# Grouped DoubleRow matmuls, norms spread through DRAM, and a merged last load group in a fused attention and feed-forward kernel

## The chip, the cores and the metric

The kernel runs on one core of a Trainium2 chip. In the profiles PE is TensorE, which does the matmuls, and PEld its weight loads; the program puts their results in PSUM banks (`g_ps`, `v_ps` and others, two of each of these). DVE (VectorE), ACT (ScalarE) and POOL (GpSimd) do the element-wise work, SP issues DMAs. A DMA "lands" when its data has arrived, and "[0.30 <-X]" after a line says that the engine sat idle for 0.30 us before it, until X ended. The metric is the device time in microseconds of one execution. The profile of an execution also gives its span, from the first to the last instruction, which is some 1.8 us shorter than the time.

## The reference

```python
qn = q / (norm(q, axis=1) + 1e-6)          # q, k, v: (4, 6016, 256), tau = 1
kn = k / (norm(k, axis=1) + 1e-6)
s = kn.transpose(0, 2, 1) @ qn / tau       # 256 x 256 per batch
a = softmax(s)                             # over the last axis
x = (v @ a).reshape(24064, 256)
out = (silu(x @ w_gate) * (x @ w_val)) @ w_out     # 256 -> 1536 -> 256
```

## The kernel before

The kernel folds the attention matrix into the feed-forward weights (`Wg`, `Wv`), so the main loop is three matmul groups per step: `g_ps`, `v_ps` (512 columns each, two matmuls each) and four of the output product `o_new` (256 columns). ScalarE makes `silu`, VectorE multiplies it with `v_ps`. A step takes 1.30 us of TensorE.

Beside these steps, a plan spreads the next batch's attention over the loop: squares for the norms, the raw product of q and k in fp8 (`gemm1_pair`, with DoubleRow, a mode in which one fp8 matmul takes two 128-row blocks), the norms, the logits, the softmax, the new weights. The parts that the change touches:

```python
def gemm1_pair(b, t):                     # one pair of 128-row blocks, two halves
    ...
    for jh in range(CH):
        nc.tensor.matmul(kq[:, jh, :], q_sb[:, ps:ps + 2, js], k_sb[:, ps:ps + 2, :],
                         ..., perf_mode=DR)          # the last block alone: plain fp8

def norm_cols(b):                         # sums of squares -> inverse norms, one per partition
    ...
    nc.gpsimd.tensor_tensor(out=inv, in0=inv, in1=minus, op=ALU.pow)
    state[b, "inv"] = inv
    parts = split3(inv[:, CH:], [P, CH], "ink")      # three bf16 parts
    ...                                              # and back to fp32 scalars, "scal"
def norm_diag(b):                         # 6 scaled identities on VectorE
    ...
def norm_rows(b):                         # 3 matmuls: ones x diag = k's norms in every row
    for i in range(3):
        nc.tensor.matmul(ps, ones_bf, state[b, "diag"][:, i], start=(i == 0), stop=(i == 2))
    nc.vector.tensor_copy(ink, ps)

for t in range(NP):                       # 24 pairs per batch
    step = SQ0 + (5 * t) // 2
    plan[step].append((norm_acc, t))
    plan[step + 1].append((gemm1_pair, t))
...
plan[S1 + 10].append((norm_cols,))
plan[S1 + 20].append((norm_diag,))
plan[S1 + 22].append((norm_rows,))
plan[S1 + 24].append((logits, 0))
```

The first batch has nothing to hide behind. Its k and q are loaded in groups, squared, multiplied and summed as they land. The v and weight loads queue behind them.

## Time and profile before

| | before |
|---|---|
| time, median of 3 runs | 815.24 us (815.13 to 815.67) |
| span of the profiled run | 813.4 us, granted clock 1.0 |
| TensorE busy | 98% |
| VectorE, ScalarE, GpSimd busy | 65%, 53%, 33% |
| TensorE idle before the first use of w_gate's second part | 0.30 us at 40.68 us |

A matmul's duration in this profile is its latency, and matmuls overlap, so what one costs in a full stream is the distance between starts: 216 ns for 512 columns, 109 ns for 256.

### The profile page before, as it was taken

How to read it: one execution, taken by the hardware profiler on the slowest of the kernel's cores; microseconds unless marked ns; L12 is line 12 of the kernel's file. 1: busy time of each engine (PE TensorE's matmuls, PEld its weight loads, DVE VectorE, ACT ScalarE, POOL GpSimd, SP SyncE). 2: the span in 40 equal slices, each digit the busy share in tenths (PEclk: the TensorE clock that was granted, in tenths of full speed). 3: DMA queues.
4: the chain of work that ended last, by engine and by line, in shares of the span. 5: the costliest groups of instructions: out<-in, count | busy, mean ns of one | idle time of the engine just before them, and what ended most of it. 6: DMA issues, size and time to landing. Idle time of an engine off the chain costs nothing.

```text
span 813.4 us, 13803 instructions
## 1 busy us (share of the span) xinstructions
PE 800.5 (98%) x5051; PEld 487.1 (60%) x5051; DVE 526.9 (65%) x816; ACT 434.9 (53%) x757; POOL 266.9 (33%) x345
## 2 busy tenths in 40 slices
PE   5999999999999999999999999999999999999998
PEld 3656666665565666666565666666656565665656
DVE  4777777667556777756756687765765555555554
ACT  4666655545555656545555566555554544544543
POOL 5515887313000888722000398751300000000000
PEclk9999999999999999999999999999999999999999
DMA  9993875328312678333813278532662112112101
GB/s 87 142 160 69 112 105 88 78 53 122 79 40 46 96 101 105 75 65 87 127 40 59 38 101 119 92 78 66 139 98 66 46 47 59 53 39 65 50 27 59
DMA packets 93507, 64.59 MB, mean 79 GB/s; under 512 B 52752, under 2 KB 92304, under 8 KB 92688
## 3 DMA queue, kind: packets, MB, share of 16 engines
q0 software_dynamic: 19344, 27.01, 28.6%
q1 hardware_dynamic: 73952, 36.65, 18.5%
q8 instruction: 39, 0.64, 0.3%
q14 instruction: 28, 0.23, 0.1%
q10 hardware_dynamic: 144, 0.07, 0.0%
HBM read 78.64 MB, written 36.70 MB: 142 GB/s over the span
## 4 chain that ended last, share of the span: by engine, by line
PE 95%; DMA 4%; POOL 0%; issue 0%; DVE 0%; POOLq 0%
PE o_new L474 30%; PE g_ps L440 30%; PE v_ps L440 30%; DMA q_sb<-in_q_dram 2%; PE ps L409 2%; PE kq_new L151 2%; DMA k_sb<-in_k_dram 1%; DMA w_gate_sb<-in_moe_w_gate_dram 1%; POOL k_sb L106 0%; PE last_ps L498 0%; PE ps L334 0%; PE cs L308 0%; POOL w_val_sb L541 0%; PE kq_new L156 0%; POOL vb L114 0%
## 5 line engine op out<-in xcount | busy, mean ns | idle before, releaser
L450 DVE TENSOR_TENSOR sv<-silu,v_ps 128x512 bf16<-128x512 bf16 (+1 forms) x576 | 388.7, 675 | 262.6 <-ACT silu L446 260.8
L446 ACT ACTIVATE silu<-g_ps 128x512 bf16<-128x512 f32 (+1 forms) x576 | 338.5, 588 | 324.8 <-PE g_ps L440 299.3
L474 PE MATMUL o_new<-w_out_sb,sv 128*128 128x256 bf16 x2244 | 337.3, 273 | 0.0
L440 PE MATMUL g_ps<-vT,Wg 128*128 128x512 bf16 (+1 forms) x1128 | 331.3, 375 | 0.0
L440 PE MATMUL v_ps<-vT,Wv 128*128 128x512 bf16 (+1 forms) x1128 | 330.4, 375 | 0.0
L474 PEld LDWEIGHTS <-sv 128*128 128x128 bf16 x2244 | 219.1, 98 | 141.1
L440 PEld LDWEIGHTS <-Wv 128*128 128x128 bf16 x1152 | 112.5, 98 | 130.8
L284 POOL TENSOR_TENSOR acc_new<-acc_new,sq 128x512 f32<-128x512 f32 x135 | 158.0, 1170 | 43.2 <-DVE sq L274 33.8
L440 PEld LDWEIGHTS <-Wg 128*128 128x128 bf16 x1152 | 106.6, 98 | 27.1
L274 DVE TENSOR_TENSOR sq<-q_sb 128x512 bf16<-128x512 fp8e5 x72 | 64.5, 896 | 0.0
L279 POOL TENSOR_TENSOR acc_new<-sq 128x512 f32<-128x512 bf16 x3 | 3.5, 1152 | 150.6 <-DVE sq L274 150.6
L275 ACT ACTIVATE sq<-k_sb 128x512 bf16<-128x512 fp8e5 x72 | 44.2, 614 | 0.0
L151 PE MATMUL kq_new<-k_sb,q_sb 128*128 128x512 fp8e5 x184 | 40.1, 310 | 0.7 <-DMA q_sb<-in_q_dram 0.7
L483 ACT COPY o_sb<-o_new 128x512 f32<-128x512 f32 x48 | 28.1, 585 | 14.9 <-PE o_new L474 14.5
L106 POOL DMA_DIRECT2D q_sb<-in_q_dram x49 | 27.5, 561 | 13.6 <-DMA k_sb<-in_k_dram 5.4
L485 DVE COPY o_sb<-o_new 128x512 f32<-128x512 f32 (+1 forms) x47 | 31.3, 666 | 0.0
L106 POOL DMA_DIRECT2D k_sb<-in_k_dram x48 | 26.1, 550 | 12.1 <-DMA w_out_sb<-in_moe_w_out_dram 5.3
L178 PE MATMUL ss_new<-sq,ones_bf 128*128 128x256 bf16 x83 | 17.8, 353 | 9.3 <-ACT sq L168 8.7
L114 POOL DMA_DIRECT2D vb<-in_v_dram x47 | 24.2, 516 | 4.1 <-DMA vb<-in_v_dram 3.3
L151 PEld LDWEIGHTS <-q_sb 128*128 128x256 fp8e5 x184 | 22.2, 138 | 3.2 <-DMA q_sb<-in_q_dram 2.2
L178 PEld LDWEIGHTS <-ones_bf 128*128 128x128 bf16 x83 | 9.9, 122 | 16.0 <-issue 11.6
L354 POOL TENSOR_SCALAR den<-th 128x512 f32<-128x512 f32 x3 | 1.8, 609 | 51.8 <-ACT th L353 51.8
(101 smaller groups left out, 205.9 us busy)
## 6 DMA issues: line engine op xcount, KB each, us to landing
out_dram<-o_sb SPq DMA_DIRECT2D x92, 256.0 KB, 2.4
vb<-in_v_dram POOLq DMA_DIRECT2D x43, 256.0 KB, 5.5
k_sb<-in_k_dram POOLq DMA_DIRECT2D x44, 128.0 KB, 6.0
q_sb<-in_q_dram POOLq DMA_DIRECT2D x44, 128.0 KB, 5.0
w_out_sb<-in_moe_w_out_dram POOLq DMA_DIRECT2D x1, 768.0 KB, 13.5
vb<-in_v_dram POOLq DMA_DIRECT2D x4, 192.0 KB, 3.7
vT<-vb SPq DMA_TRANSPOSE x47, 4.3
w_gate_sb<-in_moe_w_gate_dram POOLq DMA_DIRECT2D x2, 256.0 KB, 7.0
```

The lines of the kernel that those rows point to most:

```text
L106: nc.gpsimd.dma_start(out=dst[:, gs:gs + gm, :], in_=src[b].rearrange("(p s) c -> p s c", s=NS)[:, gs:gs + gm, :])
L151: nc.tensor.matmul(kq[:, jh, :], q_sb[:, ps:ps + 2, js], k_sb[:, ps:ps + 2, :], start=(t == 0 and jh == 0), stop=last, perf_mode=DR, skip_ ...
L178: nc.tensor.matmul(state[b, "ss", which], ones_bf, sq[:, s, :], start=(t == 0 and s == 0), stop=(t == t_last and s == pm - 1))
L274: nc.vector.tensor_mul(sq[:, :pm, 0, :], q_sb[:, ps:ps + pm, :], q_sb[:, ps:ps + pm, :])
L275: nc.scalar.activation(sq[:, :pm, 1, :], k_sb[:, ps:ps + pm, :], ACT.Square)
L284: nc.gpsimd.tensor_tensor(out=acc, in0=acc, in1=sq[:, s, :, :], op=ALU.add)
L440: nc.tensor.matmul(dst[:, :mv], W[:, kk, fs], vT[:, kk, :mv], start=(kk == 0), stop=(kk == CH - 1))
L446: nc.scalar.activation(silu[:, :mv], g_ps[:, :mv], ACT.Silu)
L450: nc.vector.tensor_mul(sv[:, f, :mv], silu[:, :mv], v_ps[:, :mv])
L474: nc.tensor.matmul(self.o_ps[:, j % 2, :], self.sv[:, f, j * P:(j + 1) * P], w_out_sb[:, f, :], start=(f == 0), stop=(f == FH - 1))
L483: nc.scalar.copy(o_sb[:, :m, :], self.o_ps[:, :m, :])
L485: nc.vector.tensor_copy(o_sb[:, :m, :], self.o_ps[:, :m, :])
```

## The change

It has three parts: two pairs of the q-k product are issued together; k's inverse norms reach all partitions by a write to DRAM and a broadcast read, in place of scaled identities and three matmuls; and in the first batch the last two groups of q are handled as one, so that all q-k matmuls precede the last column sums.

```diff
         state[b, "inv"] = inv
-        parts = split3(inv[:, CH:], [P, CH], "ink")
-        ...                                  # scal, norm_diag and norm_rows go
+        row = dram.tile([C], FP32, tag="ink_row")
+        nc.gpsimd.dma_start(out=row.rearrange("(h p) -> p h", p=P), in_=inv[:, CH:])
         ink = work.tile([P, C], FP32, tag="ink")
-        nc.vector.tensor_copy(ink, ps)
+        nc.gpsimd.dma_start(out=ink, in_=row.partition_broadcast(P))
...
         plan[step].append((norm_acc, t))
-        plan[step + 1].append((gemm1_pair, t))
+        if t % 2 == 1:
+            plan[step + 1].append((gemm1_pair, t - 1))
+            plan[step + 1].append((gemm1_pair, t))
...
-    plan[S1 + 20].append((norm_diag,))
-    plan[S1 + 22].append((norm_rows,))
...
-        ts = range(gs // 2, (gs + gm + 1) // 2)
+        ts = list(range(gs // 2, (gs + gm + 1) // 2))
+        if which == 0 and g == NQ - 1:
+            continue
+        if which == 0 and g == NQ - 2:
+            gs, gm = gl[g + 1]
+            ts += range(gs // 2, (gs + gm + 1) // 2)
```

More of the change, by code (lines that the diff above doesn't have):

```diff
@@ L315, in norm_cols @@
         state[b, "inv"] = inv
-        parts = split3(inv[:, CH:], [P, CH], "ink")
-        scal = work.tile([P, 3, CH], FP32, tag="scal")
-        for i, part in enumerate(parts):
-            nc.gpsimd.tensor_copy(scal[:, i, :], part)
-        state[b, "scal"] = scal
-    def norm_diag(b):
-        scal = state[b, "scal"]
-        diag = work.tile([P, 3, CH, P], BF16, tag="diag")
-        for i in range(3):
-            for h in range(CH):
-                nc.vector.tensor_scalar_mul(diag[:, i, h, :], in0=ident,
-                                            scalar1=scal[:, i, h:h + 1])
-        state[b, "diag"] = diag
-    def norm_rows(b):
-        ps = psum_m.tile([P, C], FP32, tag="misc")
-        for i in range(3):
-            nc.tensor.matmul(ps, ones_bf, state[b, "diag"][:, i], start=(i == 0),
-                             stop=(i == 2))
+        row = dram.tile([C], FP32, tag="ink_row")
+        nc.gpsimd.dma_start(out=row.rearrange("(h p) -> p h", p=P), in_=inv[:, CH:])
         ink = work.tile([P, C], FP32, tag="ink")
-        nc.vector.tensor_copy(ink, ps)
+        nc.gpsimd.dma_start(out=ink, in_=row.partition_broadcast(P))
         state[b, "ink"] = ink
```

## The prediction

> **What bounds the kernel now.** I read the page first: the busy shares, then the chain that ended last, then the waits.
>
> ```profile
> span 813.4 us, 13803 instructions
> PE 800.5 (98%) x5051; PEld 487.1 (60%) x5051; DVE 526.9 (65%) x816; ACT 434.9 (53%) x757; POOL 266.9 (33%) x345
> ...
> PE 95%; DMA 4%; POOL 0%; issue 0%; DVE 0%; POOLq 0%
> ```
>
> TensorE is busy for 98% of the span and is 95% of the chain that ended last; DMA is 4%, all of it before 41 us. VectorE and GpSimd, where much of the change works, are at 65% and 33%. Busy alone doesn't say that TensorE runs without gaps, so I looked at its timeline in a stretch where the next batch's q-k product (L151) runs beside the feed-forward part:
>
> ```profile
> 66.64 0.60 PE L474 MATMUL o_new<-w_out_sb,sv 128*128 128x256 bf16 x4
> 66.99 0.46 PE L151 MATMUL kq_new<-k_sb,q_sb 128*128 128x512 fp8e5 x2
> 67.30 0.61 PE L440 MATMUL g_ps<-vT,Wg 128*128 128x512 bf16 x2
> 67.74 0.59 PE L440 MATMUL v_ps<-vT,Wv 128*128 128x512 bf16 x2
> 68.17 0.60 PE L474 MATMUL o_new<-w_out_sb,sv 128*128 128x256 bf16 x4
> 68.61 0.60 PE L440 MATMUL g_ps<-vT,Wg 128*128 128x512 bf16 x2
> 69.04 0.59 PE L440 MATMUL v_ps<-vT,Wv 128*128 128x512 bf16 x2
> 69.47 0.60 PE L474 MATMUL o_new<-w_out_sb,sv 128*128 128x256 bf16 x4
> ```
>
> The first column is the start, the second the busy time; the durations overlap, so starts are to be compared. A step without L151 goes from 68.17 to 69.47, 1.30 us. A step with it goes from 66.64 to 68.17, 1.53 us. So one pair of L151 matmuls costs 0.23 us, in full, on the engine that sets the end. I then compared, over all records from 40.6 us to the end, the distance between consecutive matmul ends with the rate given below. It fits within a nanosecond on average except in three kinds of place: one wait at 40.68 us (0.30 us), a surcharge of 15.1 ns in the mean each of 69 times when TensorE goes from L151 to g_ps, and some ten to twenty ns after each group of one-column matmuls. From 41 us on, therefore, a matmul that is taken away shortens the run by its spacing, and work on the other engines is free until it delays TensorE. Before that, a DMA ends the chain:
>
> ```profile
> 34.10 6.53 DMA w_gate_sb<-in_moe_w_gate_dram
> 40.68 1.04 PE ps L409 x4
> ```
>
> **What the Trainium skill says.** "TensorE: Matmul & The Clock Gate", section "Wait — 56ns, not 53.3ns?", gives a warm spacing of N ÷ 2.4 GHz + about 2.5 ns: 109.2 ns for 256 columns, 215.8 ns for 512. The trace agrees: four of 512 and four of 256 make 1.300 us, the step measured above. The same page, "Weight-path perf modes", says that DoubleRow's weight load takes 72% longer and turns the fast load off. The trace shows 138 ns against 98 ns, 41% longer. With four in a row at the start of the kernel (33.76 us, 0.63 us for four, of which the first one's own time is 0.30) the spacing is still 0.11 us, so the longer load doesn't show inside a run of them. "DMA: Bandwidth & Descriptors", "Two DMAs through the same engine are not ordered", asks for the first DMA's completion before the second is issued. The built program does this on GpSimd's queue. Its "Anatomy of one DMA" gives about 2.0 us fixed cost; the trace's smallest stores (64 KB) land in 1.5 to 2.0 us and its loads, often queued, in 4 to 6.
>
> **Part 1, two pairs of the q-k product at a time.** The number of matmuls stays the same: 23 DoubleRow pairs and one last half pair per batch, three batches. Only the returns from DoubleRow to bf16 become fewer. Before, 69 returns × 15.1 ns = 1.04 us. Afterwards the instruction order shows 12 groups per batch, of which 11 end with a DoubleRow pair and the last ends with the plain half pair (whose return costs nothing in the trace). That removes 33 returns for certain, and the three last ones if the change from DoubleRow to plain fp8 is free: 33 to 36 × 15.1 ns = **0.50 to 0.54 us**. The 0.44 us group itself can't starve anything: each g and v bank has a twin. The even pairs no longer lengthen their own step, which takes 0.23 us from the slack between the read of a v bank and its reuse; in the steady state the least of these slacks at a step concerned is 0.53 us (v_ps at 479.6 us), so 0.30 us remains.
>
> **Part 2, the inverse norms by way of DRAM.** It removes these groups:
>
> ```profile
> L327 DVE TENSOR_SCALAR diag<-ident,scal 128x128 bf16<-128x128 bf16 x18 | 3.2, 247 | 0.0
> L334 PE MATMUL ps<-diag,ones_bf 128*128 128x256 bf16 x9 | 1.5, 273 | 0.0
> L337 DVE COPY ink<-ps 128x256 f32<-128x256 f32 x3 | 1.3, 417 | 0.0
> L319 POOL CAST scal<-lo 128x2 f32<-128x2 bf16 x3 | 0.6, 190 | 0.0
> ```
>
> (columns: count, then busy us and mean ns of one, then idle before). On TensorE it is 9 matmuls, and their worth is the spacing, not the 273 ns latency: 9 × 109.2 ns = **0.98 us**. The 4.5 us of VectorE and some 4 us of small GpSimd operations lie beside TensorE and are worth nothing. Added are two DMAs per batch. GpSimd ends the last power at 166.96 us in the first batch; VectorE first reads the norms at 183.05 us. The window is 16.1 us, and 15.7 once the three matmuls of L334 between them are gone. Two legs, each an issue of about 0.6 us and a landing of 2 to 6 us (read from the loads and stores above, and one behind the other), come to 5 to 13 us. So the landing is expected at 172 to 180 us, unseen. The v load behind them on GpSimd slips by a few us; its transposed tile has about 24 us between landing and first use.
>
> **Part 3, the first q's last two groups as one.** TensorE does the last q-k product before the column sums, so one or two mode changes go, perhaps 0.03 to 0.1 us up to the softmax. But every gain up to 40.4 us runs into the w_gate transfer shown above, which landed at 40.63 us and was issued when an earlier load had landed, whatever TensorE does. TensorE already waits 0.30 us for it; it would only wait longer. Worth **0**.
>
> Sum: 0.98 + 0.52 + 0 = 1.5 us, so 815.24 − 1.5 = **813.7 us**, 0.2%.
>
> **Rivals.** (a) The norms arrive late. VectorE is in order, so its first logits operation would hold up the product behind it, and TensorE would stop once the two v banks are full. For it: many 4-byte writes to DRAM, one DMA that must land before the next is issued, and a queue shared with loads. Against: the window of nearly 16 us, and no load outstanding on that queue at 167 us (the load before landed at 155.5). If each landing took 10 us, the norms would come at 188 us, 5.5 us late; the second bank hides about 1 us of it, and three batches lose 13.5 us: 827 us. I give it 4%. (b) The surcharge belongs to each DoubleRow pair and not to the return, or grows with a longer run because 138 ns loads can't keep up with 109 ns matmuls. Part 1 would then be worth nothing or cost up to 36 × 30 ns: 814.3 to 815.3 us. The four in a row at the start speak against it. (c) The start counts after all, because the w_gate landing shifts between runs: then up to 0.1 us more goes, 813.6 us. (d) More slack on VectorE and GpSimd speeds up TensorE: there are no gaps it could fill, so nothing.
>
> **Range and chances.** The three runs before spread over 0.54 us, all of which can come from the loads at the start. A spread of this kind on both sides and 0.5 us for rival (b) give 813.1 to 814.7 us. Two per cent is 16.3 us; no sum of the parts comes near it, and only a much worse rival (a) reaches it upward. Faster by over 2%: 0.5%; within 2%: 98%; slower: 1.5%.
>
> **What would show it.** TensorE's count should fall by 9, to 5042. No group with diag or scal should be left. A step holding two pairs should take 1.30 + 0.45 us (four × 109.2 + 15 ns) and the steps between 1.30. The wait for w_gate near 40.7 us should stay, longer by what the softmax gained. The broadcast norms should land by 180 us, and the logits should have no wait for a DMA before them. I am wrong if VectorE waits for a DMA at the logits, if TensorE shows gaps near 183, 378 and 573 us, if a double group costs more than 0.47 us, or if the time before 41 us moves by more than 0.5 us.

## The result

The changed kernel took 813.64 us in the median of 6 runs (813.54 to 814.2), the kernel before 815.34 us in 6 runs. The ratio is 0.998 (95% interval 0.9967 to 0.9993). Ratios here are the mean time of one kernel's fast runs over that of the other's in the same rounds, so they are not quite the ratio of the medians. By the limit of 2% the two are the same. The predicted time was 813.7 us.

From the page of the changed kernel (span; busy time, share and instruction counts; the engines' shares of the chain that ended last):

```profile
span 811.9 us, 13668 instructions
...
PE 794.1 (98%) x4952; PEld 488.9 (60%) x5042; DVE 524.3 (65%) x795; ACT 434.8 (54%) x757; POOL 267.2 (33%) x330
...
PE 93%; DMA 4%; issue 1%; DVE 1%; POOL 0%; ACT 0%; POOLq 0%
```

The span is 1.5 us shorter. There are 9 weight loads fewer (5051 to 5042), as there should be matmuls. Of the matmuls themselves this trace holds only 4952: 90 records are missing, mostly one every 8 us, which takes some TensorE time out of the busy sum and puts small pieces of other engines into the chain. I therefore judge by starts, and by the time from the end of the first matmul on w_gate's second part to the end of the trace, called the **tail** below. What happens at the start reaches into it only where TensorE waits later for a load or for an engine (e7, e10); in the kernels of the table below it doesn't.

TensorE's timeline of the changed kernel where a double group runs (start, busy time, then what):

```profile
67.86 0.60 PE L457 MATMUL o_new<-w_out_sb,sv 128*128 128x256 bf16 x4
...
69.16 0.60 PE L457 MATMUL o_new<-w_out_sb,sv 128*128 128x256 bf16 x4
69.51 0.68 PE L151 MATMUL kq_new<-k_sb,q_sb 128*128 128x512 fp8e5 x4
70.03 0.61 PE L423 MATMUL g_ps<-vT,Wg 128*128 128x512 bf16 x2
...
70.91 0.60 PE L457 MATMUL o_new<-w_out_sb,sv 128*128 128x256 bf16 x4
```

A plain step takes 69.16 − 67.86 = 1.30 us. The step with two pairs takes 70.91 − 69.16 = 1.75 us, so the two pairs cost 0.45 us together, where two single pairs had cost 2 × 0.233 us (each two × 109.2 ns and 15.1 ns).

The start of the kernel, in the chain of the changed kernel (start, duration):

```profile
34.03 6.52 DMA w_gate_sb<-in_moe_w_gate_dram
40.60 1.04 PE ps L392 x4
```

The same load ends the start as before. TensorE now waits 0.55 us for it.

The way through DRAM, in the second of the three batches, from GpSimd's and VectorE's timelines of the changed kernel:

```profile
361.34 0.82 POOL L318 DMA_DIRECT2D row<-inv  x1 [0.30 <-POOL inv L314]
369.69 0.59 POOL L320 DMA_DIRECT2D ink<-row  x1 [7.54 <-DMA row<-inv]
...
376.81 0.48 DVE L328 SCALAR_TENSOR_TENSOR s_new<-kq_new,inv,ink 128x256 f32<-128x256 f32 x1
```

GpSimd stands still for 7.5 us until the 1 KB has landed; only then may it issue the read. The read's landing is recorded at 375.92 us, and VectorE uses the norms 0.9 us later. In the other two batches the margins are 2.2 and 1.4 us. So the detour is hidden, but barely; in e2 below, which has the same two DMAs, the least margin is 0.45 us. The times from issue to landing over the three batches, from the views of the two lines (minimum, median, maximum; first the write, then the read):

```profile
DMA to landing us min/median/max: 8.1/8.9/9.9
...
DMA to landing us min/median/max: 4.0/4.1/6.2
```

### The profile page after: what moved, and what is told of

The parts are those of the page before. It is cut to its first block, busy times and chain, and to the rows that moved or that the text cites. A ratio compares the mean times of both kernels' runs of the same rounds, so it can differ in the third digit from the quotient of the medians.

```text
span 811.9 us, 13668 instructions
## 1 busy us (share of the span) xinstructions
PE 794.1 (98%) x4952; PEld 488.9 (60%) x5042; DVE 524.3 (65%) x795; ACT 434.8 (54%) x757; POOL 267.2 (33%) x330
## 4 chain that ended last, share of the span: by engine, by line
PE 93%; DMA 4%; issue 1%; DVE 1%; POOL 0%; ACT 0%; POOLq 0%
PE o_new L457 30%; PE v_ps L423 30%; PE g_ps L423 28%; DMA q_sb<-in_q_dram 2%; PE ps L392 2%; PE kq_new L151 2%; DMA k_sb<-in_k_dram 1%; DMA w_gate_sb<-in_moe_w_gate_dram 1%; DVE sv L433 0%; POOL k_sb L106 0%; ACT silu L429 0%; PE last_ps L481 0%; POOL vb L114 0%; DVE sq L274 0%; PE kq_new L156 0%
## 5 line engine op out<-in xcount | busy, mean ns | idle before, releaser
L423 PE MATMUL v_ps<-vT,Wv 128*128 128x512 bf16 (+1 forms) x1100 | 324.3, 374 | 2.9
L423 PE MATMUL g_ps<-vT,Wg 128*128 128x512 bf16 (+1 forms) x1074 | 319.1, 375 | 0.3
L423 PEld LDWEIGHTS <-Wg 128*128 128x128 bf16 x1152 | 109.7, 98 | 24.9
L466 ACT COPY o_sb<-o_new 128x512 f32<-128x512 f32 x48 | 28.1, 586 | 14.9 <-PE o_new L457 14.5
L151 PE MATMUL kq_new<-k_sb,q_sb 128*128 128x512 fp8e5 x184 | 32.0, 295 | 0.5 <-DMA q_sb<-in_q_dram 0.5
L151 PEld LDWEIGHTS <-q_sb 128*128 128x256 fp8e5 x184 | 21.2, 138 | 2.6 <-DMA q_sb<-in_q_dram 2.0
L312 POOL TENSOR_TENSOR inv<-inv,half 128x4 f32<-128x4 f32 x3 | 3.1, 1036 | 36.7 <-DVE inv L311 36.7
## 6 DMA issues: line engine op xcount, KB each, us to landing
w_out_sb<-in_moe_w_out_dram POOLq DMA_DIRECT2D x1, 768.0 KB, 13.7
```

The lines of the kernel that those rows point to most:

```text
L423: nc.tensor.matmul(dst[:, :mv], W[:, kk, fs], vT[:, kk, :mv], start=(kk == 0), stop=(kk == CH - 1))
L466: nc.scalar.copy(o_sb[:, :m, :], self.o_ps[:, :m, :])
```

## The experiments

Twelve kernels ran, all of them with results that passed the comparison with the reference. Tails and waits are from the instruction records of each profiled run:

| kernel | time, median us | kernel before in the same rounds | span us | tail us | TensorE's wait for w_gate us |
|---|---|---|---|---|---|
| before | 815.34 | – | 813.4 | 772.347 | 0.30 |
| changed | 813.64 | 815.34 | 811.9 | 770.865 | 0.55 |
| e1 pairs only | 815.14 | 816.26 | 812.8 | 771.851 | 0.37 |
| e2 DRAM only | 814.33 | 816.26 | 812.2 | 771.351 | 0.40 |
| e3 last groups only | 815.24 | 816.26 | 813.5 | 772.343 | 0.56 |
| e4 one run | 813.28 | 816.26 | 811.4 | 770.361 | 0.55 |
| e9 one run, runs of 8 bytes | 813.11 | 815.30 | 811.2 | 770.361 | 0.54 |

The rounds of e1 to e4 were on a chip where the kernel before ranged from 815.26 to 817.75 us, so the medians and ratios there can't separate parts of half a microsecond. The tails can.

### e1: the pairs alone

```diff
-        plan[step + 1].append((gemm1_pair, t))
+        if t % 2 == 1:
+            plan[step + 1].append((gemm1_pair, t - 1))
+            plan[step + 1].append((gemm1_pair, t))
```

> The kernel before with part 1 alone (two pairs at a time). Theory (a surcharge of 15 ns at each return from DoubleRow to bf16, 33 to 36 returns gone): 0.50 to 0.54 us faster than before. Rival (the surcharge belongs to each DoubleRow pair, or a longer run is slower): no gain, or up to 1 us slower. Rival (part 1 gives all of the 1.5 us): 1.5 us faster.

The ratio was 0.9986 (0.9974 to 0.9999). The tail became 0.496 us shorter. In the records, 33 returns from L151 to `g_ps` remain, at 15.0 ns each beyond the normal spacing, and the three passages from L151 to the plain fp8 matmul (L156) cost 14.5 ns each. So 33 surcharges went, 33 × 15.1 = 0.50 us, and the change from DoubleRow to plain fp8 is not free. Entering DoubleRow costs nothing in these records (109 ns from the output product to L151). Why leaving it costs 15 ns, no run shows.

### e2: the way through DRAM alone

The edit is the first two hunks of the change without the pairs and the merged groups.

> The kernel before with part 2 alone (inverse norms by way of DRAM). Theory (9 matmuls at 109 ns leave the TensorE stream, all else is hidden): 0.98 us faster than before, no wait of VectorE for a DMA at the logits. Rival (the norms land late, VectorE is held up): less gain than 0.98 us, a wait of VectorE or TensorE gaps near the logits.

The ratio was 0.9977 (0.9965 to 0.999). The tail became 0.996 us shorter, no wait for a DMA stands before the logits, and TensorE has no gap there. The tails of e1 and e2 add to 1.492 us; both parts together gave 1.482 us.

### e3: the merged last groups alone

> The kernel before with part 3 alone (first q's last two groups as one). Theory (every gain before 40 us runs into the wait for w_gate): the same time to within 0.1 us. Rival (the start counts): 0.1 to 0.3 us faster, with the first matmul that uses w_gate's second part starting earlier by as much.

The ratio was 0.999 (0.9976 to 1.0004), unresolved at this size. The tail is the same to 0.004 us. What the part does shows at the start: from the landing of the last q load but two to the first softmax exponential, ScalarE's first on `exT`, takes 2.66 us here and 2.83 us in e1 and e2. So the start gets 0.17 us shorter, and TensorE's wait for w_gate grows from 0.37 or 0.40 to 0.56 us: the wait takes the gain. The kernel before shows 2.91 us in the same stretch in its profiled run, where an earlier q load landed late. The lines show where the 0.17 us come from, first e1, then e3:

```profile
34.51 0.17 PEld L201 LDWEIGHTS <-sq 128*128 128x128 bf16 x4 [0.22 <-ACT sq L168]
34.62 0.38 PE L156 MATMUL kq_new<-k_sb,q_sb 128*128 128x256 fp8e5 x2
34.84 0.19 PE L201 MATMUL cols<-ones_bf,sq 128*128 128x1 bf16 x2
```
```profile
34.50 0.39 PE L156 MATMUL kq_new<-k_sb,q_sb 128*128 128x256 fp8e5 x2
34.73 0.29 PE L201 MATMUL cols<-ones_bf,sq 128*128 128x1 bf16 x6
```

In e1 the last q-k pair (L156, two matmuls of 109 ns) comes after TensorE's wait for ScalarE's last square and between the last column sums; in e3 it runs before that square is done. From the square's end to the end of the last sums it is 0.58 us in e1 (34.45 to 35.03) and 0.41 us in e3 (34.61 to 35.02). No DoubleRow matmul lies in this stretch, so the gain is the new order and not a mode change.

### e4: all 24 pairs in one run

```diff
-        if t % 2 == 1:
-            plan[step + 1].append((gemm1_pair, t - 1))
-            plan[step + 1].append((gemm1_pair, t))
+        if t == NP - 1:
+            for u in range(NP):
+                plan[step + 1].append((gemm1_pair, u))
```

> The changed kernel with all 24 pairs of a batch in one run of TensorE, at the step of the last pair. Theory (the surcharge is paid at each return, whatever the length of the run): 3 returns in place of 36, 33 x 15 ns = 0.50 us faster than the changed kernel; spacing within the run 109 ns. Rival (the longer DoubleRow weight load, 138 ns, makes a long run slower than 109 ns per matmul): 138 matmuls x up to 29 ns = up to 4 us slower. Second rival (VectorE and ScalarE run dry for 5 us and TensorE then waits for them): slower by 1 us or more, with gaps on TensorE right after the run.

Against the changed kernel the tail is 0.504 us shorter, which is 33 returns × 15 ns. TensorE's timeline of this kernel:

```profile
140.66 0.60 PE L457 MATMUL o_new<-w_out_sb,sv 128*128 128x256 bf16 x4
141.02 5.27 PE L151 MATMUL kq_new<-k_sb,q_sb 128*128 128x512 fp8e5 x46
146.12 0.39 PE L156 MATMUL kq_new<-k_sb,q_sb 128*128 128x256 fp8e5 x2
146.35 0.38 PE L423 MATMUL g_ps<-vT,Wg 128*128 128x512 bf16 x1
```

The 46 matmuls keep a spacing of 109 ns: from 141.10 us (140.66 and four output matmuls at 109 ns) to 146.12 us is 46 × 0.109 us. The surcharge belongs to leaving DoubleRow, not to a pair, and the longer weight load (138 ns) doesn't bind even over 46. TensorE goes on without a gap after it, though ScalarE and VectorE had nothing to do for 5 us.

### e5: twice as many small writes

```diff
-        row = dram.tile([C], FP32, tag="ink_row")
-        nc.gpsimd.dma_start(out=row.rearrange("(h p) -> p h", p=P), in_=inv[:, CH:])
+        row = dram.tile([2 * C], FP32, tag="ink_row")
+        nc.gpsimd.dma_start(out=row.rearrange("(h p) -> p h", p=P), in_=inv)
...
-        nc.gpsimd.dma_start(out=ink, in_=row.partition_broadcast(P))
+        nc.gpsimd.dma_start(out=ink, in_=row[C:].partition_broadcast(P))
```

> The changed kernel, the small DMA to DRAM writing 512 elements in place of 256 (q's inverse norms too, not read back). In the changed kernel its 1 KB lands 8.1 to 9.9 us after the issue. Theory A (the landing grows with the number of 4-byte writes): about 16 us to landing, the norms land after 187 us where the logits stand at 182.5 us, VectorE waits for a DMA there, and the kernel is slower by 2 us or more per batch, 6 to 12 us in all. Theory B (a fixed latency of a small write to DRAM): 8 to 10 us to landing as before and the same time within 0.1 us.

Neither theory held: the write landed in 10.5 us (two landings recorded), between the two. The time was 815.1 us in the median of 4 runs (ratio 0.9997, 0.9984 to 1.0009), 1.5 us above the changed kernel, which ran in other rounds. That is not all due to the norms: in the profiled run TensorE also ran its matmuls at twice their spacing around 36 to 39 us, which made the first use of w_gate's second part end 1.18 us later than in the changed kernel. The tail is 0.70 us longer, and this part is the norms. In the second batch they came late; in the other two they were in time by 1.4 and 1.0 us. VectorE's and then TensorE's timeline of this kernel:

```profile
379.74 0.48 DVE L328 SCALAR_TENSOR_TENSOR s_new<-kq_new,inv,ink 128x256 f32<-128x256 f32 x1 [1.68 <-DMA ink<-row]
380.14 0.68 DVE L433 TENSOR_TENSOR sv<-silu,v_ps 128x512 bf16<-128x512 bf16 x1
```
```profile
380.02 0.59 PE L423 MATMUL g_ps<-vT,Wg 128*128 128x512 bf16 x2
380.88 0.59 PE L423 MATMUL v_ps<-vT,Wv 128*128 128x512 bf16 x2 [0.26 <-DVE sv L433]
```

VectorE stood idle for 1.68 us; TensorE lost 0.42 us here and 0.29 us two steps later, 0.70 us in all, since the second bank covered the rest. This is rival (a) of the prediction at work, but the slower write alone didn't bring it about. In that batch GpSimd issued the read only at 375.73 us, 2.7 us after the write had landed at 373.00; in every other batch with a recorded landing, in all the runs, it took 0.3 us. Issued after 0.3 us, the read would have landed at about 377.2 us (an estimate from these times and the 3.9 us that it took), before VectorE came free at 378.06 us. Each of the 14 traces has exactly one such DMA issue on GpSimd, 1.6 to 2.4 us late with no wait that the profile names. In twelve of them it is the 117th or 118th DMA that GpSimd issues, a q or k load; in e5 the 108th, the read, and in e12, which also has more small writes, the 110th. So the added writes may have moved it onto the read; no run tests that, and its cause is open.

### e6: runs of 8 bytes

```diff
-        nc.gpsimd.dma_start(out=row.rearrange("(h p) -> p h", p=P), in_=inv[:, CH:])
+        nc.gpsimd.dma_start(out=row.rearrange("(p h) -> p h", p=P), in_=inv[:, CH:])
```

> The changed kernel, the small DMA writing 128 runs of 8 bytes in place of 256 runs of 4 (the order in DRAM is then wrong for the reader: a wrong result on purpose). Theory A (the landing grows with the number of separate writes): 5 to 6 us to landing in place of 8.9. Theory B (fixed latency): 8 to 10 us. The time of the kernel stays the same under both.

The single run (state unknown) took 813.63 us. The view of the write's line:

```profile
DMA to landing us min/median/max: 3.1/3.3/3.4
```

The landing is 5.6 us shorter in the median, more than halving the number of writes would explain under theory A, and against theory B. The order in DRAM was wrong for the reader, yet the result passed: presumably the norms of 6016 random values differ too little for the comparison to see a permutation of them, which no run tests. It is no proof of a right layout.

### e7 and e8: w_gate's second part ahead of a v chunk

```diff
-    load_v(*allc[1])
-    for wc in range(1, NWC):
+    load_w(WP, 2 * WP)
+    load_v(*allc[1])
+    for wc in range(2, NWC):
         load_w(wc * WP, (wc + 1) * WP)
```

> The changed kernel, with w_gate's and w_val's second part loaded ahead of the second v chunk. Theory (TensorE waits 0.56 us for w_gate near 40.6 us, and the start before it has slack): w_gate lands about 1.2 us earlier, the wait goes, 0.4 to 0.6 us faster than the changed kernel. Rival (another load, w_val or v, takes its place): less than 0.2 us faster, with a new wait for it on TensorE before 55 us.

> As the run before, without part 3 of the change (the last two groups of q apart again). With w_gate's wait gone, the start shows what part 3 is worth: theory 0.03 to 0.1 us slower than the run before; rival (part 3 does nothing, the softmax is bound by ScalarE's chain): the same within 0.03 us.

Both became slower: 821.52 us (ratio 1.0076, 1.0064 to 1.0088) and 820.28 us (1.0064, 1.0052 to 1.0076). The wait for w_gate did go. But the v chunk's transposing DMA, issued at 42.09 in place of 39.33 us, now took 16 us in place of 9, and TensorE waited for it. Both transfers overlapped the load of w_out, which itself took 17.6 us in place of 13.7; why both were slower is open. From the chain, then from TensorE's timeline of e7:

```profile
42.09 16.05 DMA vT<-vb
```
```profile
58.19 1.03 PE L423 MATMUL g_ps<-vT,Wg 128*128 128x512 bf16 x2 [5.42 <-DMA vT<-vb]
59.02 1.06 PE L423 MATMUL v_ps<-vT,Wv 128*128 128x512 bf16 x2
```

After the wait the matmuls of 512 columns run at 427 ns for some 3 us, twice the normal spacing. The rival won, and far above what it was thought to cost. With another wait in the way, the times of e7 and e8 say nothing of part 3. Up to the first exponential, e7, with part 3, needed 2.91 us and e8 2.83 us, but in e7 the last q load but three landed late (32.51 us), as in the kernel before (32.38 us).

### e9: one run, and norms in runs of 8 bytes

The edit is that of e4 and e6 together, with VectorE reading k's norms in the order in which they lie:

```diff
-            out=state[b, "s"][:, jh, :], in0=kq[:, jh, :], scalar=inv[:, jh:jh + 1],
-            in1=ink, op0=ALU.mult, op1=ALU.mult)
+            out=state[b, "s"][:, jh, :].rearrange("p (h l) -> p h l", h=CH),
+            in0=kq[:, jh, :].rearrange("p (h l) -> p h l", h=CH), scalar=inv[:, jh:jh + 1],
+            in1=ink.rearrange("p (l h) -> p h l", h=CH), op0=ALU.mult, op1=ALU.mult)
```

> The changed kernel with one run of 24 pairs per batch and the norms in DRAM as 128 runs of 8 bytes, read by VectorE in the order that they have there (a right result). Theory: the time of the kernel with one run alone, 0.50 us faster than the changed kernel, since the landing was hidden already; the norms land 5 us earlier and the margin before the logits becomes 6 to 8 us. Rival (the stride of 8 bytes makes VectorE's two logits operations slower than 0.48 us and TensorE waits): slower than the one run by 0.2 us or more.

This was the fastest kernel by its median: 813.11 us (812.97 to 813.18, ratio 0.997, 0.9958 to 0.9983). Its tail equals that of e4 to the nanosecond, so the shorter landing gained margin and no time, as expected; e4's 813.28 us was measured on another chip. VectorE's logits operation takes 476 ns as before. GpSimd's timeline in the second batch:

```profile
360.91 0.64 POOL L318 DMA_DIRECT2D row<-inv  x1 [0.30 <-POOL inv L314]
364.42 0.56 POOL L320 DMA_DIRECT2D ink<-row  x1 [2.88 <-DMA row<-inv]
```

The norms land at 369.41 us and are read at 376.38 us, a margin of 7.0 us where the changed kernel has 0.9.

### e10 and e11: other matmuls ahead of the wait

```diff
-            g_ps, v_ps, mv = gv_matmuls(b, ci, f)
+            g_ps, v_ps, mv = ahead.pop(f, None) or gv_matmuls(b, ci, f)
+            if gi == 0 and f == 1:
+                ahead[2] = gv_matmuls(b, ci, 2)
```

> The run before, with the third step's g and v matmuls ahead of the first use of w_gate's second part, so that TensorE has 0.86 us of work in place of the 0.55 us wait. Theory (the wait for w_gate ended the start): the wait goes, 0.4 to 0.55 us faster than the run before. Rival (its v bank isn't free yet, or w_val's wait takes its place): less than 0.15 us faster, with TensorE waiting for VectorE or for a DMA before 44 us.

> The run before, without part 3 of the change. With the wait for w_gate gone the start shows what part 3 is worth: theory 0.01 to 0.1 us slower from the landing of the last q to the first matmul that reads the softmax; rival (part 3 shortens the start by 0.1 to 0.3 us, hidden until now): slower by as much.

e10 took 814.18 us (ratio 0.9987, 0.9973 to 1.0001), about 1 us more than e9. TensorE's timeline:

```profile
40.48 0.59 PE L424 MATMUL g_ps<-vT_new,Wg 128*128 128x512 bf16 x2 [0.19 <-ACT silu L430]
41.20 0.59 PE L424 MATMUL v_ps<-vT_new,Wv 128*128 128x512 bf16 x2
41.63 1.02 PE L393 MATMUL ps<-w_gate_sb,exT 128*128 128x512 bf16 x4
43.07 1.02 PE L393 MATMUL ps<-w_val_sb,exT 128*128 128x512 bf16 x4 [0.41 <-DVE Wg L403]
```

The wait for w_gate is gone, but the g and v banks weren't free (0.35 and 0.29 us), and later the w_val matmuls wait 0.57 us for an evacuation: 1.21 us of waits in place of 0.54. So w_gate's load isn't the only thing that holds the start; ScalarE's and VectorE's evacuations stand right behind it. The experiment's rival held.

e11, the same with part 3 undone, took 814.23 us. From the last q landing but two to the first exponential it needs 2.84 us, e10 2.66, and the first matmul on w_gate's second part ends 0.37 us later; 0.18 of it is part 3, the rest a later landing of q (34.00 and 33.80 us for the last one but one). The medians, 0.05 us apart with spreads over 1 us, don't resolve it.

### e12: 4-byte writes that lie apart

```diff
+        apart = dram.tile([C, 16], FP32, tag="ink_apart")
+        nc.gpsimd.dma_start(out=apart.rearrange("(h p) o -> p h o", p=P)[:, :, 0:1],
+                            in_=inv[:, CH:].rearrange("p (h o) -> p h o", o=1))
```

> The changed kernel with one more small DMA after the two: the same 256 writes of 4 bytes, each into a 64-byte stretch of DRAM of its own, read by nobody. Theory C (4-byte writes are slow where neighbours from several DMA engines fall into one 64-byte stretch): 3 to 4 us to landing. Theory D (a 4-byte write is slow by itself): 8 to 10 us. The time of the kernel stays the same under both, as the DMA is off the path.

In the single run (813.77 us, state unknown) the views of the two write lines show, first the packed row, then the one spread out:

```profile
DMA to landing us min/median/max: 8.8/9.3/10.8
...
DMA to landing us min/median/max: 2.7/3.2/4.3
```

The same 256 writes of 4 bytes from the same source land in a third of the time where each has 64 bytes of DRAM to itself. So a 4-byte write isn't slow by itself; theory D falls. That neighbours written by different DMA engines hold each other up (theory C) fits this, but no run isolates it. In e6 there are still neighbours within 64 bytes; the theory covers e6 only if one DMA engine writes them there, which no trace shows.

## Why the prediction was right

**TensorE sets the time from 41 us on, and a removed matmul is worth its spacing.** Shown: e2 took 9 matmuls away and the tail shrank by 0.996 us, against 0.98. The 4.5 us taken from VectorE gave nothing beyond that.

**15 ns per return from DoubleRow.** Shown by e1 (0.496 us, forecast 0.50 to 0.54) and by e4, where 33 further returns went and 0.504 us with them. The open end of the range closed at its lower side: DoubleRow to plain fp8 costs 14.5 ns. That these are marks of the mode and not of the profile's modelled matmul ends is shown by the tails, which shrink by the same sums. Rival (b) falls by e4.

**Part 3 is worth nothing in the end.** Shown by e3's tail and wait. Its size up to the softmax was set too low, 0.03 to 0.1 us against 0.17 to 0.18 us measured, because it was put down to mode changes; the lines of e3 show that the order of the last q-k pair and ScalarE's last square matters more. The mechanism that makes it worth nothing, a wait for w_gate that takes it all, was right in the kernel as it stands. That the path would have been free without this wait isn't so: e10 shows the next waits behind it.

**The norms land unseen.** Right in the outcome, with the landing term mis-sized. "A landing of 2 to 6 us" for each leg should have been 8.1 to 9.9 us for the write and 4.0 to 6.2 us for the read. (It also added the issue to a landing time that is counted from the start of the issue, a small slip the other way.) The sum of 5 to 13 us was 13 to 15 us in a window of 15.7, and "172 to 180 us" in the first batch was 180.24 us. The estimate was drawn from loads and large stores; the trace before had no write of 4-byte pieces to draw on. That this still fitted was partly luck: the margins were 0.9 to 2.2 us, and 0.45 us in e2, so 4% for rival (a) was low. In e5 one late issue was enough, and its cost was 1.68 us on VectorE and 0.70 us on TensorE; the second bank hid 1.0 us, as the prediction had it.

**The sum.** 1.5 us was forecast; the tail gives 1.48 us. The medians differ by 1.70 us. Of the remaining 0.2 us, 0.08 us is w_gate's earlier end in the profiled run; the rest lies within the spread of the runs.

## What to carry to other kernels

Where one engine runs without gaps, price a removed instruction by the distance between starts, look for surcharges where its mode changes, and group the work of one mode into as few runs as its data allows. Before an operation is hidden behind a DMA, ask what the DMA's pieces look like in memory and not how many bytes it moves, and check the margin in every batch. A gain ahead of a wait is worth nothing, and taking the wait away may only show the next one.

## What the Trainium skill lacked or had wrong

- "TensorE: Matmul & The Clock Gate", section "Weight-path perf modes": it doesn't tell of a cost of leaving DoubleRow. The runs show 15 ns at each return to bf16 and 14.5 ns from DoubleRow to plain fp8.
- The same section: it gives DoubleRow's weight load as 72% longer and its matmul as 13% longer, measured at 512 columns. Here, at 256 columns, the load is 138 ns against 98 ns, 41% longer, and the matmuls keep the bf16 spacing of 109 ns over 46 in a row. Whether the 13% is meant of the spacing the page doesn't say.
- "DMA: Bandwidth & Descriptors", sections "Anatomy of one DMA" and "Specifications": a fit of about 2 us plus the bytes over the bandwidth for one DMA, and a remark that transfers under 512 B are done by read-modify-write. Here 1 KB in 256 packed writes of 4 bytes took 8.0 to 10.8 us to landing, in 128 runs of 8 bytes 3.1 to 3.6 us, and in 256 writes of 4 bytes set 64 bytes apart 2.7 to 4.3 us. The page advises against short pieces, but no page has a landing time for pieces of 4 or 8 bytes.
- No page has a figure for it: a transposing DMA issued 2.8 us later took 16 us in place of 9 (e7), with a 768 KB load beside it in both cases.
